# Moving the tiles that hold x's operands to other byte offsets in SBUF (linear attention, RMS norm, SiLU feed-forward)

## The chip, the cores and the metric

One Trainium2 chip, one of its cores. The metric is the device time of one execution in microseconds, the median over several runs.

## What is computed

```python
kv  = einsum('bhsd,bhse->bhde', k, v)                 # 8 x 8 heads, 576 rows, 64 wide
o   = einsum('bhsd,bhde->bhse', q, kv)
o   = o / sqrt(mean(o*o, -1) + 1e-6) * g_norm
x   = o.transpose(0, 2, 1, 3).reshape(4608, 512)
h   = x @ w_in                                         # 512 -> 2048
out = (h * sigmoid(h)) @ w_out                         # 2048 -> 512
```

Everything is float32.

## The kernel before

**Split numbers.** The large products run on TensorE in the type fp32r. To keep float32 accuracy each operand is split into an upper part in fp32r and a lower part, the rest. A product is then three matmuls into one accumulator: upper by lower, lower by upper, upper by upper. Every such matmul has a 128x128 *stationary* operand, loaded by its own LDWEIGHTS, and a *moving* operand of 512, 288 or 256 columns that streams through it. In the rows a matmul reads `out<-a,b` with its shapes `stationary moving`.

**Stages.** The 4608 tokens are nine tiles of 512 (NT = 9). `x` of a tile is stored transposed, as four chunks of 128 features by 512 tokens, each with its upper and lower part. The hidden layer is 16 blocks of 128 (NF = 16). For a block the first product (w_in, line 468 in `products`, or line 636 in `product`) has a block of w_in as stationary operand and x as moving operand; then SiLU on ScalarE and the split on VectorE make the tiles `gh` and `gl`; then the second product (w_out, line 499 in `project`) has `gh` or `gl` as stationary operand and the block of w_out (512 columns) as moving operand, into four accumulator banks.

- Token tile 0: x is in the tiles `x0` to `x3`, made by `x_part`. `x0` to `x2` lie in the three slots `spare0` to `spare2`, `x3` in the slot `late0`.
- Token tile 1: x is in the one tile `x_second`. In tiles 0 and 1 a block is 12 matmuls of line 468 (512 columns), then 12 of line 499 (512 columns).
- Token tiles 2 to 8: the first product runs as seven products of half size (Strassen-Winograd, functions `make_operand`, `product`, `pair_step`), each of six matmuls with 256 moving columns. Two blocks make one pair step, and there are 8 pair steps in each of the seven tiles, 56 in all. The moving operands of products 4, 7, 2 and 3 lie in `x_second` (it has four chunks of 4 KB for them), those of products 1, 6 and 5 in the tiles `operand4` to `operand6`, which have taken over the slots `spare0` to `spare2`. Between the products stand matmuls of line 499, in groups of three: one group after products 1 and 6, two after 5 and 4, three after 7 and 2, the rest after 3. They belong to the pair step before.
- The attention (lines 247 to 297) of the next batch is spread over the steps in between. Its output product (lines 282, 283, 284 in `mm_out`) takes three matmuls of 288 columns: stationary `kh`, `kl`, `kh`, moving `ql`, `qh`, `qh`, first on the left half of the 576 columns, then on the right half.

The order of the instructions is written out by hand in lists (`first_jobs`, `mid_jobs`, `last_jobs`), one place for each step; nothing in it depends on addresses.

**Where the tiles lie.** A tile takes a fixed stretch of bytes in each of the 128 partitions. The pools lie one after the other, `const` first, and within it the slots lie in the order in which they are first asked for, each rounded up to 32 bytes. What matters here is the start of each slot, in bytes, and its rest by 256:

```
slot                      start    rest by 256   holds
kvm0..3, kh (2 slots)      1152 ..  128          attention, kh: stationary, lines 282, 284
kl (2 slots)               4288 ..  192          stationary, line 283
x_second                   5344     224          moving, line 468 (tile 1), line 636 (products 4, 7, 2, 3)
spare0, spare1, spare2    21728 ..  224          moving, line 468 (x0..x2), line 636 (products 1, 6, 5)
late1, late0              34016 ..  224          x in float32, w_out in float32; late0 first holds x3
32 weight blocks          42208 ..  224          w_in: stationary, w_out: moving, sums of w_in: stationary
q, k, v, qh, ql           173280 .. 224          moving, lines 282 to 284: left half 224, right half 224+1152, rest 96
gh, gl                    214240 .. 224          stationary, line 499
```

Rows within the tiles are 512, 1024 or 2048 bytes apart, so that every operand of lines 468, 499 and 636 has the rest 224 as well, stationary or moving.

The diff touches `late`, which is called for the slots `late0` and `late1`, and the lines around line 106 where `x_second` is made.

Of the kernel before, what the change touches and what calls it, by code (L numbers as in the profile page):

```python
# [8 lines left out]
F32 = mybir.dt.float32  # L9
# [21 lines left out]
def linear_attention_rms_silu_ffn(  # L31
# [23 lines left out]
    B, NP, P, S = q.shape  # L55
# [9 lines left out]
    const = ctx.enter_context(tc.tile_pool(name="const", bufs=1))  # L65
# [37 lines left out]

    x_second = const.tile([P, NP, 2, TN], F32R, name="x_second")
    x_first, lates = {}, {}

    def spare(n, shape, dtype, name):
        return const.tile(shape, dtype, name=name, tag=f"spare{n}")  # L110

    def late(n, shape, dtype, name):
        if name not in lates:
            lates[name] = const.tile(shape, dtype, name=name, tag=f"late{n}")
        return lates[name]

    def x32(c, w):

        return late(c // 2, [P, 2, TN], F32, f"x32_{c // 2}")[:, c % 2, w]
# [14 lines left out]
    def full_tile(kind, f):  # L134
        if kind == "wo":
            t = late(1, [P, 2, NP * P], F32, "wo_full")[:, f % 2]
        else:
            t = tmp.tile([P, S], F32, name="full", tag="tmp")[:, :NP * P]
        fulls[kind, f] = t
        return t  # L140
# [54 lines left out]
    def x_part(t, a, c):  # L195

        if t == 1:
            return x_second[:, c, a]
        if c not in x_first:
            kind = {"shape": [P, 2, TN], "dtype": F32R, "name": f"x{c}"}  # L200
            x_first[c] = spare(c, **kind) if c < 3 else late(0, **kind)
        return x_first[c][:, a]
# [598 lines left out]
    with tc.manual_schedule():  # L801
# [4 lines left out]
        for item in ORDER.split():  # L806
            kind, n = item.rstrip("0123456789"), int(item.lstrip("wiopbg") or 0)
# [234 lines left out]
```

## Time and profile before

| | |
|---|---|
| median of 3 runs | 846.33 us (846.32 to 846.63) |
| the profiled execution | 846.25 us |
| its span, first to last instruction | 844.5 us |
| PE busy | 834.0 us, 99% of the span |
| VectorE, ScalarE, GpSimd busy | 537.1, 431.0, 290.3 us |
| clock that TensorE was granted | 1.00 of full speed throughout |

The profiled execution is 1.75 us longer than its span, and 0.08 us below the median of the runs. PE is TensorE's matmul side, PEld its weight loads, which overlap the matmuls. Matmuls overlap too: one starts while the one before drains, so the time that one takes up is the distance from its start to the start of the next, here called its *pitch*, and not its duration. In a timeline row that merges several matmuls (`x12`), the start of the next row less the start of this one, over 12, is their mean pitch.

### The profile page before, as it was taken

What the parts mean: (1) busy time and instruction counts of PE and PEld (TensorE: products, weight loads), DVE (VectorE), ACT (ScalarE), POOL (GpSimd) and SP (SyncE); (2) the same over time, 40 slices, a digit from 0 to 9 for tenths busy, and PEclk for the clock granted to TensorE, in tenths of its full rate; (3) what the DMA queues carried; (4) which work ended last, traced back from release to release, by engine and by line L of the source; (5) the groups of instructions that cost most, each with busy time, mean ns of one, the idle gap of its engine ahead of it and who ended that gap; (6) DMA issues with size and microseconds to landing.
All of it is one profiled execution on the core that took longest, in us unless ns stands there. A gap on an engine that the chain in (4) does not pass through costs nothing.

```text
span 844.5 us, 14347 instructions
## 1 busy us (share of the span) xinstructions
PE 834.0 (99%) x5454; PEld 740.3 (88%) x5454; DVE 537.1 (64%) x1067; ACT 431.0 (51%) x957; POOL 290.3 (34%) x254
## 2 busy tenths in 40 slices
PE   8999999999999999999999999999999999999998
PEld 8667888888899999999999999999999999999997
DVE  4886866774676567756766577666765763464333
ACT  4766554333664457446654465456644544454443
POOL 2776884620332223222422242223322222222220
DMA  8779011241322332232314331232211121112111
GB/s 326 304 259 358 1 57 54 98 176 61 106 76 79 134 106 101 76 131 78 111 51 134 120 116 51 85 126 83 100 50 51 50 101 50 51 51 100 51 51 50
DMA packets 33205, 89.01 MB, mean 105 GB/s; under 512 B 3824, under 2 KB 4080, under 8 KB 33136
## 3 DMA queue, kind: packets, MB, share of 16 engines
q1 hardware_dynamic: 33136, 88.10, 29.7%
q8 instruction: 43, 0.70, 0.3%
q14 instruction: 26, 0.21, 0.1%
HBM read 74.45 MB, written 13.63 MB: 104 GB/s over the span
## 4 chain that ended last, share of the span: by engine, by line
PE 94%; DMA 4%; POOL 1%; ACT 0%; issue 0%; SPq 0%
PE acc L499 46%; PE hp L636 33%; PE hp L468 9%; PE at L247 2%; DMA wo<-in_moe_w_out 1%; DMA k<-in_k 1%; DMA early_wi<-in_v 1%; PE at L284 1%; PE at L283 1%; PE at L282 1%; DMA v<-in_v 1%; PE at L499 1%; DMA wi<-in_moe_w_in 1%; PE at L280 1%; POOL wo L185 0%
## 5 line engine op out<-in xcount | busy, mean ns | idle before, releaser
L499 PE MATMUL acc<-wo,gh 128*128 128x512 f32 (+1 forms) x1152 | 357.1, 391 | 0.1
L580 POOL TENSOR_TENSOR wi<-wi,wi 128x512 fp32r<-128x512 f32 x112 | 145.2, 1297 | 420.2 <-ACT wi L579 417.2
L499 PEld LDWEIGHTS acc<-wo,gh 128*128 128x128 f32 x1152 | 201.4, 189 | 29.0 <-POOL wo L185 0.3
L499 PE MATMUL acc<-wo,gl 128*128 128x512 f32 x576 | 222.7, 387 | 0.5 <-POOL gl L479 0.5
L636 PEld LDWEIGHTS hp<-x_second,wi 128*128 128x128 f32 x1344 | 179.9, 191 | 9.0
L636 PE MATMUL hp<-x_second,wi 128*128 128x256 f32 x1344 | 187.7, 282 | 0.0
L636 PEld LDWEIGHTS hp<-operand,wi 128*128 128x128 f32 x1008 | 135.3, 190 | 9.0
L636 PE MATMUL hp<-operand,wi 128*128 128x256 f32 x1008 | 138.3, 282 | 0.0
L499 PEld LDWEIGHTS acc<-wo,gl 128*128 128x128 f32 x576 | 108.2, 188 | 24.1 <-POOL gl L479 1.0
L579 ACT CAST wi<-wi 128x512 fp32r<-128x512 f32 x112 | 69.0, 616 | 107.2 <-DMA wi<-sums_in_dram 105.3
L692 DVE TENSOR_TENSOR wi<-hp,wi 128x256 f32<-128x256 f32 x56 | 23.8, 425 | 145.9 <-PE hp L636 145.9
L643 ACT ACTIVATE gh<-gf 128x512 fp32r<-128x512 f32 x56 | 35.4, 632 | 127.4 <-DVE gf L693 127.4
L647 DVE TENSOR_TENSOR gl<-wi,gh 128x256 fp32r<-128x256 f32 x112 | 48.4, 432 | 30.7 <-ACT wi L644 28.0
L269 POOL TENSOR_TENSOR ql<-q,qh 128x576 fp32r<-128x576 f32 x24 | 34.4, 1433 | 67.2 <-ACT qh L268 56.7
L643 ACT ACTIVATE gh<-wi 128x256 fp32r<-128x256 f32 x112 | 45.9, 410 | 15.0 <-DVE wi L708 14.9
L647 DVE TENSOR_TENSOR gl<-gf,gh 128x512 fp32r<-128x512 f32 x56 | 38.7, 690 | 20.9 <-ACT gf L644 20.1
L477 ACT ACTIVATE gh<-hp 128x512 fp32r<-128x512 f32 x31 | 18.5, 597 | 61.4 <-PE hp L468 61.4
L644 ACT ACTIVATE wi<-wi 128x256 f32<-128x256 f32 x112 | 46.8, 418 | 3.5
L468 PE MATMUL hp<-x,wi 128*128 128x512 f32 x180 | 45.7, 399 | 1.4 <-POOL wi L185 1.4
L468 PE MATMUL hp<-x_second,wi 128*128 128x512 f32 x192 | 46.4, 390 | 0.0
L468 PEld LDWEIGHTS hp<-x_second,wi 128*128 128x128 f32 x192 | 35.7, 188 | 7.3
L468 PEld LDWEIGHTS hp<-x,wi 128*128 128x128 f32 x180 | 33.2, 188 | 9.0 <-POOL wi L185 1.8
(140 smaller groups left out, 1024.8 us busy)
## 6 DMA issues: line engine op xcount, KB each, us to landing
wi<-sums_in_dram SPq DMA_DIRECT2D x56, 512.0 KB, 3.3
out<-ob SPq DMA_DIRECT2D x35, 256.0 KB, 2.4
wi<-in_moe_w_in SPq DMA_DIRECT2D x16, 512.0 KB, 7.9
wo<-in_moe_w_out SPq DMA_DIRECT2D x16, 512.0 KB, 8.8
k<-in_k SPq DMA_DIRECT2D x28, 288.0 KB, 4.6
v<-in_v SPq DMA_DIRECT2D x28, 288.0 KB, 4.7
q<-in_q SPq DMA_DIRECT2D x28, 288.0 KB, 3.6
sums_in_dram<-sums SPq DMA_DIRECT2D x8, 512.0 KB, 2.6
```

Source lines behind the costliest of these rows:

```text
L247: nc.tensor.matmul(out=self.kv[h], lhsT=self.k[rows, c, :], rhs=self.v[rows, c, :], start=(start and r == 0), stop=(stop and r == 4),)
L269: nc.gpsimd.tensor_tensor(out=self.ql, in0=self.q, in1=self.qh.bitcast(F32), op=ALU.subtract)
L468: nc.tensor.matmul(out=hp[:, :TN], lhsT=w[:, a, fs], rhs=x_part(t, b, c), start=(c == 0 and i == 0), stop=(c == NP - 1 and i == 2),)
L477: nc.scalar.activation(out=gh, in_=hp[:, :TN], func=AF.Silu)
L499: nc.tensor.matmul(out=bank, lhsT=g[:, ns], rhs=w[:, a, cs], start=(f == first and i == 0), stop=(f == last and i == 2))
L579: nc.scalar.copy(out=two[:, 0], in_=raw)
L580: nc.gpsimd.tensor_tensor(out=two[:, 1], in0=raw, in1=two[:, 0].bitcast(F32), op=ALU.subtract)
L636: nc.tensor.matmul(out=out, lhsT=a_of(i, a, c), rhs=x[:, b, c], start=(n == 0), stop=(n == 5))
L643: nc.scalar.activation(out=gh[:, w], in_=x, func=AF.Silu)
L644: nc.scalar.activation(out=x, in_=x, func=AF.Silu)
L647: nc.vector.tensor_tensor(out=gl[:, w], in0=x, in1=gh[:, w].bitcast(F32), op=ALU.subtract)
L692: nc.vector.tensor_tensor(out=u3, in0=v, in1=u2, op=ALU.add)
```

## The change

Three tiles that nothing reads or writes are put between the others: 128 bytes ahead of `x_second`, 64 bytes behind it, and 64 bytes ahead of the first slot that `late` asks for.

```diff
+    def gap(n):
+
+        const.tile([P, n // 4], F32, name=f"gap{n}")
+
+    gap(128)
     x_second = const.tile([P, NP, 2, TN], F32R, name="x_second")
+    gap(64)
     x_first, lates = {}, {}
 ...
     def late(n, shape, dtype, name):
+        if not lates:
+            const.tile([P, 16], F32, name="gap_late")
         if name not in lates:
             lates[name] = const.tile(shape, dtype, name=name, tag=f"late{n}")
         return lates[name]
```

By the layout above `x_second` then starts at 5472 (rest 96), the three spare slots at 21920 and on (rest 160), and `late1` at 34272 (rest 224). All that lies behind moves up by 256 bytes and keeps its rest. No instruction is added, removed or reordered.

## Rows read from the trace of the kernel before

**Rows 1.** Page: busy time, share of the span and instructions of each engine.

```profile
PE 834.0 (99%) x5454; PEld 740.3 (88%) x5454; DVE 537.1 (64%) x1067; ACT 431.0 (51%) x957; POOL 290.3 (34%) x254
```

**Rows 2.** Page: the chain that ended last, by engine.

```profile
PE 94%; DMA 4%; POOL 1%; ACT 0%; issue 0%; SPq 0%
```

**Rows 3.** Windows: busy time by engine, then granted clock, DMA share, GB/s.

```profile
0.00:50.00 50.00, 44.16 (x325) 37.03 (x326) 34.59 (x66) 29.91 (x63) 26.86 (x43) 1.00 0.83 309
...
180.00:800.00 620.00, 620.00 (x4175) 560.20 (x4174) 389.06 (x805) 319.83 (x718) 166.93 (x127) 1.00 0.26 89
```

**Rows 4.** Groups of PE's instructions, shapes apart: count, busy us, mean ns of one.

```profile
L499 PE MATMUL acc<-wo,gh 128*128 128x512 f32 x1120 | 350.8, 394 | 0.1
L636 PE MATMUL hp<-x_second,wi 128*128 128x256 f32 x1344 | 187.7, 282 | 0.0
L636 PE MATMUL hp<-operand,wi 128*128 128x256 f32 x1008 | 138.3, 282 | 0.0
L468 PE MATMUL hp<-x_second,wi 128*128 128x512 f32 x192 | 46.4, 390 | 0.0
```

**Rows 5.** PE timeline, token tile 1: start us, us, line, operands, count.

```profile
198.99 2.88 PE L468 MATMUL hp<-x_second,wi 128*128 128x512 f32 x12
201.71 0.39 PE L499 MATMUL acc<-wo,gh 128*128 128x512 f32 x1
```

**Rows 6.** PE timeline, one pair step of a later tile.

```profile
453.04 0.63 PE L499 MATMUL acc<-wo,gh 128*128 128x512 f32 x2
...
454.43 1.59 PE L636 MATMUL hp<-operand,wi 128*128 128x256 f32 x12
455.86 0.63 PE L499 MATMUL acc<-wo,gh 128*128 128x512 f32 x2
...
456.56 0.87 PE L636 MATMUL hp<-operand,wi 128*128 128x256 f32 x6
457.26 0.88 PE L636 MATMUL hp<-x_second,wi 128*128 128x256 f32 x6
457.98 0.63 PE L499 MATMUL acc<-wo,gh 128*128 128x512 f32 x2
```

**Rows 7.** Groups of PE in 456.5 to 457.25, then 457.255 to 457.97.

```profile
L636 PE MATMUL hp<-operand,wi 128*128 128x256 f32 x6 | 0.9, 281 | 0.0
...
L636 PE MATMUL hp<-x_second,wi 128*128 128x256 f32 x6 | 0.9, 283 | 0.0
```

**Rows 8.** PE timeline: attention's output product, left half, then right half.

```profile
247.94 0.29 PE L282 MATMUL at<-ql,kh 128*128 128x288 f32 x1
248.07 0.29 PE L283 MATMUL at<-qh,kl 128*128 128x288 f32 x1
248.20 0.29 PE L284 MATMUL at<-qh,kh 128*128 128x288 f32 x1
248.34 0.63 PE L499 MATMUL acc<-wo,gh 128*128 128x512 f32 x2
...
251.09 0.29 PE L282 MATMUL at<-ql,kh 128*128 128x288 f32 x1
251.22 0.30 PE L283 MATMUL at<-qh,kl 128*128 128x288 f32 x1
251.36 0.30 PE L284 MATMUL at<-qh,kh 128*128 128x288 f32 x1
251.50 0.62 PE L499 MATMUL acc<-wo,gh 128*128 128x512 f32 x2
...
252.87 0.28 PE L636 MATMUL hp<-operand,wi 128*128 128x256 f32 x1
```

**Rows 9.** PE timeline, token tile 1, behind attention's output product.

```profile
141.97 2.92 PE L468 MATMUL hp<-x_second,wi 128*128 128x512 f32 x12
144.72 0.29 PE L282 MATMUL at<-ql,kh 128*128 128x288 f32 x1
```

**Rows 10.** One tile's instructions, 320 to 360 us: duration ns min/median/max.

```profile
L636 PE MATMUL hp<-operand,wi x65: 277/283/283, 319.8 to 356.4; 128*128 128x256 f32 x65
```

## Prediction

> **What bounds the kernel now.** I read the page's busy times first, then the chain, then the windows, then PE's groups and timelines. TensorE is busy 99% of the span [rows 1] and makes up 94% of the chain that ended last [rows 2]; the rest of the chain is mostly the DMAs of the start. Between 180 and 800 us PE is busy 620.00 of 620.00 us, at a granted clock of 1.00, while VectorE is busy 389 and ScalarE 320 us of it [rows 3]. So in three quarters of the span nothing but the pitch of the matmuls sets the time, and a nanosecond per matmul is worth microseconds: lines 636 and 468 hold 1344 + 1008 + 192 matmuls with x moving [rows 4], and 180 more with x0 to x3.
>
> The change touches no instruction, so the whole question is whether the pitch depends on where in SBUF the operands start. The reader should look at the pitch, then. In token tile 1 twelve matmuls of 512 columns take 2.72 us, 226.7 ns each [rows 5]. In the later tiles six of 256 columns take 0.72 us, 120.0 ns each (from 457.26 to 457.98) [rows 6]. The difference, 106.7 ns, is what 256 columns cost; so beside its columns each matmul takes 13.3 ns more, in both sizes alike. I call this the locked pitch. In both runs the moving and the stationary operand have the same rest of 224.
>
> The pitch is not always the locked one, and that is what the forecast rests on. (a) The six matmuls on `operand6` that follow three of line 499 have a mean duration of 281 ns, the six on `x_second` right behind them 283 [rows 7]; the shortest of a run has 277 [rows 10]. Durations move with the pitch, so these are 2 and 6 ns under the locked pitch. (b) Matmuls of 512 columns that come right behind a run of 256 columns are slower: six take 1.39 us, three take 0.70 us [rows 6], where the locked pitch makes 1.36 and 0.68. (c) Attention's three matmuls of 288 columns take 0.40 us with the rest 224 of the left half and 0.41 us with the rest 96 of the right half, with the same stationary tiles and the same work ahead of them; the line-499 matmuls behind the right half take 1.37 us for six [rows 8], not the 1.39 of (b). All 24 pairs of halves show one of two such patterns, 20 of them this one. So a moving operand's start does move the pitch, by nanoseconds.
>
> **The change part by part.** *The three gaps themselves.* They are written and read by nothing: no instruction, no wait, no transfer, cost 0. What lies behind the third gap moves by 256 bytes and keeps its rest, the weights, gh, gl, q and k among it. `x3` too: it lies in `late0`, behind the third gap, and stays at 224, so 45 of the 180 matmuls on x0 to x3 see no new rest.
>
> *256 columns, 2352 matmuls.* Their moving operands get the rests 96 and 160, against 224 of their stationary ones. No row has x moving at another rest. Below, the nearest row is (a)'s first-of-a-run, 6 ns less for every one: -14.1 us. Above, it is (c), 0.01 us in three matmuls, 3.3 ns more for every one: +7.8 us. I take (a)'s 281 against 283, -2 ns, or -4.7 us: 283 is the largest duration in [rows 10] and at once its median, so the locked pitch is the slowest that these matmuls show, and whatever breaks the lock has more room below than above.
>
> *512 columns of line 499 in the later tiles.* A pair step has four runs of them, of 3, 6, 9 and 6; 56 steps make 224 runs. Each now pays 0.02 to 0.03 us at its entry (b). Behind the right half it pays 0.01 (c). If another rest of x changed the entry in this way throughout, that would be -0.02 x 224 = -4.5 us; at worst the entry is that of [rows 9], where twelve take 2.75 us (+0.03), at no gain. I take half the gain, -2.2 us.
>
> *Tiles 0 and 1.* Here x and w_out alternate in runs of twelve, all locked [rows 5]. With different rests each switch may start a transient such as [rows 9] show behind attention's matmuls, 0.03 us. 32 blocks make 64 switches; some 48 lie behind the first 50 us, in which PE has idle time that hides them (44.16 us busy of 50 [rows 3]). 48 x 0.03 = +1.4 us, ends 0 and +1.9.
>
> *The other engines.* ScalarE and VectorE write these tiles at the new starts. Both have idle time in every window [rows 3] and PE waits for neither there; were each of the writes 2% slower it would still be hidden. If PE gets 5 us faster over 620, the others' shares rise by 1%, which makes nothing late.
>
> *Sum.* -4.7 - 2.2 + 1.4 = -5.5 us. From the profiled execution's 846.25 us, which is 0.08 us below the median of the runs, that is 840.8 us.
>
> *Two rules to weigh.* The rows show 13.3 ns beside the columns [rows 5, 6]. The Trainium skill, "TensorE: Matmul & The Clock Gate", section "Wait — 56ns, not 53.3ns?", gives a warm matmul a fixed cost of about 2.5 ns beside its columns; here the trace shows 10.8 ns more than that, and an estimate by that page, with all of it gone in 2352 matmuls, is -25.4 us, 820.9 us. Rows 8 show that the moving operand's start matters at all. The Trainium skill, "SBUF — State Buffer", section "Who interferes with whom", says that PE has two read ports, one for the moving operand and one for weight loads, independent of each other, and that PE never waits on anyone; by that the relative start could not matter and the change would be worth 0. The trace disagrees by its 0.01 us in three matmuls.
>
> **The rivals.**
> - *No effect.* What counts may be only the rest by 32 or 64, which stays what it was (224, 96 and 160 are all 32 behind a multiple of 64). For it: the locked 13.3 ns are the same for x_second, operands and weights moving, at every row inside the tiles. Against it: (c), where 224 and 96 differ. The SBUF page's two ports would give the same. Time 846.3, own range 844.7 to 848.
> - *A slower lock.* x_second at rest 96 settles on a slower pitch than at 224, as the right half does: 3.3 ns on its 1344 + 192 matmuls, +5.1 us, 851.4. It decides from the first run of x_second in tile 1, from 130 us on, and is steady through the kernel. For it: 0.41 against 0.40 us in 20 of 24 pairs. Against it: the three there never settle, their stationary rests are 128 and 192, and the run behind them gains back as much. Own range 848 to 856.
> - *Most of the 13.3 ns goes.* The fixed part comes from the moving and the stationary operand being read at equal rests, and parting them takes it away: 6.5 ns (120.0 less the 113.5 that [rows 10]'s 277 stands for) in 2352, -15.3 us, 831. For it: such a pitch does occur. Against it: only at a run's start; and three matmuls of 288 columns take 0.40 us with unequal rests, which by 106.7 ns per 256 columns leaves 13 ns each.
>
> **How the numbers follow.** The forecast case, some faster, has 0.42 (own range 836.5 to 844.5), most of it gone 0.06, no effect 0.24, slower lock 0.28. Faster by over 0.2% (1.7 us, about what a measurement of this kernel can tell from no change): 0.42 + 0.06 = 0.48; same 0.24; slower 0.28. The cases have both signs, so the range must hold them: 833 to 853.5 leaves out most of the 0.06 and the dearer third of the slower lock, 0.14 in all.
>
> **What would show it.** Right: PE's groups of line 636 fall from 282 to about 280 ns, both x_second and operand; runs of six of line 499 in the later tiles fall below 1.39 us; the twelves of tile 1 rise above 2.72 us; PE stays busy without a gap from 180 to 800 us. No effect: 2.72, 0.72 and 1.39 us unchanged. Slower lock: x_second's group of line 636 rises above 283 while operand's doesn't. If the two groups part, rests 96 and 160 differ, and the sum has to be made for each. The prediction fails altogether if gaps appear in PE's timeline, or if the groups of line 499 move by more than the entries of their runs.

## The result, and the profile after

The changed kernel takes 847.38 us, median of 20 runs (847.07 to 847.71); the kernel before took 846.25 beside it (20 runs, 845.93 to 846.63). The ratio is 1.0014, 95% interval 1.0007 to 1.0020: 1.13 us slower, which is clear of the interval but within the 0.2% that the prediction named as no change. The forecast was 840.8, 5.5 us faster. The profiled spans are 845.3 us after and 844.5 before.

The page's busy times, its chain of waits and the window from 180 to 800 us, in the columns of [rows 1 to 3]:

```profile
PE 835.2 (99%) x5454; PEld 737.2 (87%) x5454; DVE 537.2 (64%) x1067; ACT 431.0 (51%) x957; POOL 290.1 (34%) x254
...
PE 94%; DMA 4%; POOL 1%; issue 0%; ACT 0%; SPq 0%
```

```profile
180.00:800.00 620.00, 620.00 (x4171) 557.20 (x4170) 389.87 (x808) 319.93 (x718) 166.03 (x127) 1.00 0.26 89
```

PE is still busy without a gap at a granted clock of 1.00, the other engines have the same busy times, and PE has 1.2 us more. So nothing moved but the pitch, as foreseen; it only moved the other way. PE's groups, shapes apart, answer to [rows 4] (line 644 is what 636 was, 476 was 468, 507 was 499). The first row is of before, the others are of after:

```profile
L499 PE MATMUL acc<-wo,gl 128*128 128x512 f32 x560 | 218.2, 390 | 0.5 <-POOL gl L479 0.5
...
L507 PE MATMUL acc<-wo,gh 128*128 128x512 f32 x1120 | 350.5, 394 | 0.1
L507 PE MATMUL acc<-wo,gl 128*128 128x512 f32 x560 | 220.7, 394 | 0.5 <-POOL gl L487 0.5
L644 PE MATMUL hp<-x_second,wi 128*128 128x256 f32 x1344 | 188.2, 283 | 0.0
L644 PE MATMUL hp<-operand,wi 128*128 128x256 f32 x1008 | 135.3, 279 | 0.0
L476 PE MATMUL hp<-x_second,wi 128*128 128x512 f32 x192 | 47.3, 395 | 0.0
```

The two groups of line 644 part: `operand`, now at rest 160, falls from 282 to 279 ns; `x_second`, now at 96, rises from 282 to 283. The group of 512 columns on `x_second` rises from 390 to 395, that of `gl` in line 499 from 390 to 394. Tile 1 and a pair step, in the columns of [rows 5] and [rows 6]:

```profile
200.36 2.96 PE L476 MATMUL hp<-x_second,wi 128*128 128x512 f32 x12
203.15 0.63 PE L507 MATMUL acc<-wo,gh 128*128 128x512 f32 x2
```

```profile
454.65 0.63 PE L507 MATMUL acc<-wo,gh 128*128 128x512 f32 x2
...
456.04 1.54 PE L644 MATMUL hp<-operand,wi 128*128 128x256 f32 x12
457.42 0.63 PE L507 MATMUL acc<-wo,gh 128*128 128x512 f32 x2
...
458.82 0.88 PE L644 MATMUL hp<-x_second,wi 128*128 128x256 f32 x6
459.53 0.63 PE L507 MATMUL acc<-wo,gh 128*128 128x512 f32 x2
...
462.36 0.64 PE L507 MATMUL acc<-wo,gh 128*128 128x512 f32 x2
...
464.46 0.88 PE L644 MATMUL hp<-x_second,wi 128*128 128x256 f32 x6
```

Read them by the starts. The twelve of tile 1 take 2.79 us where they took 2.72. Twelve on `operand` take 1.38 (456.04 to 457.42) where they took 1.43: here the gain is. Six on `x_second` take 0.71, hardly less than the 0.72 before. The nine of line 507 behind `x_second` take 2.10 (462.36 to 464.46); nine at the locked pitch would take 2.04. The instructions on `x_second` before and after and on `operand` after, in 320 to 360 us (minimum, median and maximum duration), beside [rows 10]:

```profile
L636 PE MATMUL hp<-x_second,wi x90: 277/283/283, 322.2 to 359.9; 128*128 128x256 f32 x90
...
L644 PE MATMUL hp<-x_second,wi x78: 279/282/292, 323.7 to 358.7; 128*128 128x256 f32 x78
...
L644 PE MATMUL hp<-operand,wi x72: 276/281/281, 320.5 to 358.0; 128*128 128x256 f32 x72
```

No duration was above 283 before; now `x_second` reaches 292. By the single starts its pitch goes 117, 120, 123, 117, 120, 123 ns, a mean of 120, with durations up to 285; the 292 are 25 matmuls that stand last in a run, right ahead of attention's, at a pitch of 130. `operand` mostly goes 116, 118, 119, 116, 114, 113, 114, 113 and stays at 113.3.

### The profile page after: what moved, and what is told of

The parts are those of the page before. It is cut to its first block, busy times and chain, and to the rows that moved or that the text cites. A ratio compares the mean times of both kernels' runs of the same rounds, so it can differ in the third digit from the quotient of the medians.

```text
span 845.3 us, 14347 instructions
## 1 busy us (share of the span) xinstructions
PE 835.2 (99%) x5454; PEld 737.2 (87%) x5454; DVE 537.2 (64%) x1067; ACT 431.0 (51%) x957; POOL 290.1 (34%) x254
## 4 chain that ended last, share of the span: by engine, by line
PE 94%; DMA 4%; POOL 1%; issue 0%; ACT 0%; SPq 0%
PE acc L507 46%; PE hp L644 33%; PE hp L476 9%; PE at L255 2%; DMA wi<-in_moe_w_in 1%; DMA wo<-in_moe_w_out 1%; DMA k<-in_k 1%; PE at L291 1%; PE at L292 1%; PE at L290 1%; DMA early_wo<-in_k 1%; PE at L507 1%; DMA early_wo<-in_q 1%; PE at L288 1%; POOL wo L193 0%
## 5 line engine op out<-in xcount | busy, mean ns | idle before, releaser
L507 PE MATMUL acc<-wo,gl 128*128 128x512 f32 x576 | 225.2, 391 | 0.5 <-POOL gl L487 0.5
L644 PEld LDWEIGHTS hp<-operand,wi 128*128 128x128 f32 x1008 | 133.0, 188 | 9.3
L644 PE MATMUL hp<-operand,wi 128*128 128x256 f32 x1008 | 135.3, 279 | 0.0
```

Source lines behind the costliest of these rows:

```text
L507: nc.tensor.matmul(out=bank, lhsT=g[:, ns], rhs=w[:, a, cs], start=(f == first and i == 0), stop=(f == last and i == 2))
L644: nc.tensor.matmul(out=out, lhsT=a_of(i, a, c), rhs=x[:, b, c], start=(n == 0), stop=(n == 5))
```

## The experiments

For after and the kernels run on the whole problem I added up the pitch (the next matmul's start less this one's) over every matmul of a group, and took off the same sum of the kernel before. In us; the *difference* is from here on the moving operand's rest less the stationary one's, and the *entry* of a run is what its first matmuls take over the locked pitch:

```
group (matmuls)         after    e1     e2     e5     e8    e10    e11    e12    e14
operand, 256 (1008)     -2.90  -0.60  -1.49  -3.68  -1.42  -1.10  -1.49  -1.49  -1.20
x_second, 256 (1344)    +0.53  +0.17  -0.54  -3.62  -2.39  -1.74  -2.06  -2.05  -3.02
x, 512, tiles 0 and 1   +1.70  +1.03  +0.79  +1.91  +0.48  +0.96  +1.89  +0.79  +0.05
w_out, 512 (line 499)   +1.84  +0.76  -0.26  +4.71  +0.72  +1.15  -3.27  -3.41  -2.42
all of PE               +0.86  +1.32  -1.48  -1.07  -2.82  -0.54  -4.91  -5.98  -6.59
timed against before    +1.13  +1.30  -1.36  -1.01  -2.94  -0.70  -4.90  -6.06  -6.65
```

The last two rows agree within 0.3 us everywhere: the pitch is nearly the whole of the time.

**Each part alone, and the rests without a difference (e1 to e4).** e1 has `x_second` at 96 and the rest of before everywhere else; e2 has only the spare slots (x0 to x2, operand4 to operand6) at 160. e3 and e4 shift the stationary tiles too, by one gap ahead of everything: all at 96, all at 0.

```diff
 # e1
+    const.tile([P, 32], F32, name="gap_ahead")
     x_second = const.tile([P, NP, 2, TN], F32R, name="x_second")
+    const.tile([P, 32], F32, name="gap_behind")
 # e2
     x_second = const.tile([P, NP, 2, TN], F32R, name="x_second")
+    const.tile([P, 48], F32, name="gap_behind")
...
+        if not lates:
+            const.tile([P, 16], F32, name="gap_late")
 # e3 ([P, 32]) and e4 ([P, 8])
+    const.tile([P, 32], F32, name="gap_ahead")
     x_second = const.tile([P, NP, 2, TN], F32R, name="x_second")
```

> Only x_second moves, to the rest 96; the spare slots and all else stay at 224. Theory A (each matmul's pitch follows from the rest of its own moving operand against that of the stationary operand, so the two moves add up): line 636 on x_second +0.5 us, line 468 on x_second +0.9, line 636 on operand 0, line 499 takes +1 to +2; in all 848 to 849.5, slower than before. Theory B (what counts is that the two kinds of x tiles differ from each other, so one move alone is as good as both): operand's mean falls from 282 to 279 ns here too, 847.4. Theory C (chance, or other engines' writes): nothing moves by more than 0.3 us in any group, 846.3.

> Only the spare slots move, to the rest 160; x_second and all else stay at 224. Theory A: line 636 on operand -2.9 us (mean 279 ns), line 468 on x0 to x3 +0.8, line 636 on x_second and line 468 on it 0 (282 and 390 ns), line 499 within 0.5; in all 844 to 844.7, faster than before by 0.2%. Theory B: as with both moved, 847.4. Theory C: 846.3.

> One gap of 128 bytes ahead of x_second alone: x's tiles, the weights, q, k, v, gh and gl all get the rest 96, so moving and stationary operands of lines 468, 499 and 636 have equal rests again; only kh, kl and the masked k*v tiles keep theirs. Theory A1 (only the difference of the two rests counts): as before, 282 ns in line 636 and 2.72 us for twelve of tile 1, 846.3. Theory A2 (the moving operand's own rest counts): x_second as in the changed kernel, 283 ns and 2.77 us or more for twelve, and line 499's 512 columns too, 2000 matmuls by some 5 ns, 852 to 856.

> One gap of 32 bytes ahead of x_second: all of those operands start at a multiple of 256. Theory A1 (only the difference of the rests counts): as before, 120.0 and 226.7 ns locked, 846.3. Theory A2 (the own rest counts, above all whether an operand starts on a multiple of 64 or more): the fixed part beside the columns falls from 13.3 ns to less, in all 4400 matmuls with 256 or 512 columns; at 6.7 ns, the least that a run's first matmul showed, -29 us, 817.

Measured: e1 847.54 us against 846.24, ratio 1.0014 (1.0005 to 1.0024); e2 844.88, 0.9984 (0.9974 to 0.9993); e3 847.22, 1.0011 (1.0002 to 1.0021); e4 846.64, 1.0005 (0.9996 to 1.0015). PE's groups of e1, then of e2:

```profile
L638 PE MATMUL hp<-x_second,wi 128*128 128x256 f32 x1344 | 187.8, 282 | 0.0
L638 PE MATMUL hp<-operand,wi 128*128 128x256 f32 x1008 | 137.7, 281 | 0.0
L470 PE MATMUL hp<-x_second,wi 128*128 128x512 f32 x192 | 47.3, 395 | 0.0
```

```profile
L639 PE MATMUL hp<-x_second,wi 128*128 128x256 f32 x1344 | 187.2, 282 | 0.0
L639 PE MATMUL hp<-operand,wi 128*128 128x256 f32 x1008 | 136.7, 281 | 0.0
L471 PE MATMUL hp<-x_second,wi 128*128 128x512 f32 x192 | 46.4, 390 | 0.0
```

The expectations held in sign alone: e1 lies below Theory A's 848 to 849.5, and e2 is 0.2 us above its 844 to 844.7, with half of the gain forecast on `operand` (-1.49 us, mean 281, not 279). Theory B had e1's time, but e2 refutes it (847.4 forecast), and the groups refute Theory C. e4 can't be told from no change; e3 is 0.98 us slower, far from the 852 to 856 of Theory A2.

The two parts have opposite signs. `x_second` at 96 costs, above all in the 512 columns of tile 1 (395 against e2's 390) and behind it in line 499; the spare slots at 160 gain. The timeline of e4, tile 1 and a later tile:

```profile
198.91 2.88 PE L469 MATMUL hp<-x_second,wi 128*128 128x512 f32 x12
201.63 0.62 PE L500 MATMUL acc<-wo,gh 128*128 128x512 f32 x2
...
457.46 0.88 PE L637 MATMUL hp<-x_second,wi 128*128 128x256 f32 x6
458.18 0.63 PE L500 MATMUL acc<-wo,gh 128*128 128x512 f32 x2
```

2.72 and 0.72 us, as before, with all of it at rest 0 in place of 224. So a rest by itself does nothing to these runs; the difference counts. By the sums of pitches e3 and e4 lose 0.7 and 0.6 us in line 499 and at most 0.11 in any group on x's tiles. The loss is all behind attention's 288 columns, whose kh and kl kept their starts, so that the differences there did change.

e1 and e2 together make -0.1 us, the change +1.13: the parts don't add, against Theory A. The intervals of these times are wide for that, but the groups show it as well (line 499 has +0.76 and -0.26 by themselves, +1.84 together). The single starts show where. Twelve on `operand` behind line 499 come to 1413 ns in e2 (each 117 to 119) and to a mean of 1381 after the change (mostly 113.3 from the sixth on); nine of line 499 behind `x_second` take 27.5 ns over the locked pitch before and in e2, 44 in e1 and 52 after. The changed kernel has both cycles in itself: of its 56 runs of twelve on `operand`, 40 take 1376 or 1377 ns and 11 take 1413 or 1414. So the same matmuls with the same starts settle on one cycle or another; that the runs before decide it is the likeliest reading, but no run tried it by itself.

**One difference for every moving operand (e5 to e8).** Here w_out's blocks, which move in line 499, are shifted with x: all moving operands -64, -32, -96 or +64 from their stationary ones.

```diff
 # e5; e6, e7 and e8 have 8 and 56, 24 and 40, 48 and 16 in place of 16 and 48
+    between.tile([P, 16], F32, name="gap_between")
...
+    const.tile([P, 48], F32, name="gap_ahead")
     x_second = const.tile([P, NP, 2, TN], F32R, name="x_second")
...
-        return weights.tile([P, 2, NP * P], dtype, name=f"{kind}{f}", tag=f"{kind}{f}")
+        pool = weights_out if kind == "wo" else weights
+        return pool.tile([P, 2, NP * P], dtype, name=f"{kind}{f}", tag=f"{kind}{f}")
...
```

> The blocks of w_out get a pool of their own, so that all moving operands of lines 468, 499 and 636 (x's tiles, w_out) have the rest 160 and all stationary ones (w_in, its sums, gh, gl) 224: every load of stationary weights now differs from the running matmul's moving operand by the same -64. Theory A (the difference of rests sets the pitch): the 113.3 ns that operand's second products reached at this difference holds everywhere, 6.7 ns less in 2352 matmuls of 256 columns (-15.7 us); if the 512-column ones gain as much, another -13.7; 817 to 833. Theory D (any uniform difference locks at 13.3 ns beside the columns; only a change of difference between runs unlocks it): 282 ns in line 636 and 2.72 us for twelve of tile 1 as before, 845 to 847.

> As the kernel with -64, with all moving operands at 192, a difference of -32. Theory A: a pitch of its own, between 113 and 123 ns for 256 columns, so 830 to 853; nothing measured says which. Theory D: 845 to 847.

> As the kernel with -64, with all moving operands at 128, a difference of -96. Theory A: between the -64 of the spare slots (113 to 118 ns) and the -128 of x_second (117, 120, 123 in turn): 116 to 120 ns, 836 to 846. Theory D: 845 to 847.

> As the kernel with -64, with all moving operands at 32 of the next 256, a difference of +64. Theory A with a sign (what counts is who leads): not the -64 kernel's time, 840 to 855. Theory A without a sign (what counts is the distance alone): within 1 us of the kernel with -64. Theory D: 845 to 847.

Measured against 846.31: e5 845.30, 0.9989 (0.9980 to 0.9999); e6 851.70, 1.0064 (1.0049 to 1.0079); e7 852.05, 1.0068 (1.0053 to 1.0083); e8 843.37, 0.9964 (0.9950 to 0.9979). PE's groups of e5:

```profile
L505 PE MATMUL acc<-wo,gh 128*128 128x512 f32 x1120 | 352.4, 396 | 0.0
L642 PE MATMUL hp<-x_second,wi 128*128 128x256 f32 x1344 | 184.1, 280 | 0.0
L474 PE MATMUL hp<-x_second,wi 128*128 128x512 f32 x192 | 47.5, 396 | 0.0
```

The large gain hoped for at -64 (817 to 833) didn't come: 256 columns gain 7.3 us, but 512 columns lose 6.6 by the table. The time lies in Theory D's 845 to 847, but its rows don't: it had 282 ns and 2.72 us unchanged, and the means are 280 and 396. e6 fits Theory A's wide range; e7 was expected at 836 to 846 and missed it. By their sums of pitches, made as for the table, e6 and e7 gain only 1.3 and 3.0 us in the 256 columns and lose 6.9 and 8.9 in the 512. e8 was to be within 1 us of e5 if the sign didn't count; it is 1.9 us faster, so the sign counts too. The two widths want different differences, which no theory until then had.

**The pitch by itself (e9).** None of the reference is computed: runs of 36 matmuls with one moving tile at each difference, on two stationary tiles of the same rest in turn. It is a single execution; from 15 to 190 us PE is at a granted clock of 1.00 throughout.

> The disputed pitch by itself: none of the reference is computed; runs of 36 matmuls, each with its weight load, one moving tile for each difference of the rests (0, 16, 32, 64, 96, 128, 160, 192, 224), with 512 and with 256 columns; then with half the stationary columns (64, differences 0, 64, 128); then in bfloat16 (0, 64). Theory A (the load of the next weights and the running matmul collide in SBUF, by their difference): 512 columns 226.7 at 0, 229 at 64, 233 to 234 at 128 to 224; 256 columns 120 at 0, 113 or 118 at 64 and 192, 120 at 128; with 64 stationary columns half of the 13.3 ns beside the columns; in bfloat16 at most 3 ns beside them and no difference between 0 and 64. Theory E (the 13.3 ns are a fixed cost of changing weights, and differences only matter through the order in the kernel): the same pitch at every difference, 13.3 ns with 64 columns and in bfloat16 too.

Measured, settled pitch (the mean of the last 24 pitches of a run) in ns:

```
difference          0     16     32     64     96    128    160    192    224
512 columns     226.7  231.7  233.3  228.9  233.3  233.3  234.5  233.3  233.3
256 columns     120.0  118.6  116.7  113.3  120.0  118.8  117.4  113.3  118.3
bf16, 512       215.8                215.8
bf16, 256       109.2                109.2
```

Lines of e9's timeline, each for a run of 36 (the next start less this one, over 36, holds the entry as well):

```profile
15.14 8.32 PE L57 MATMUL f512x<-m0x,st 128*128 128x512 f32 x36
23.30 8.50 PE L57 MATMUL f512x<-m16x,st 128*128 128x512 f32 x36
31.64 8.57 PE L57 MATMUL f512x<-m32x,st 128*128 128x512 f32 x36
...
90.32 4.48 PE L57 MATMUL f256x<-m0x,st 128*128 128x256 f32 x36
94.63 4.44 PE L57 MATMUL f256x<-m16x,st 128*128 128x256 f32 x36
...
103.11 4.24 PE L57 MATMUL f256x<-m64x,st 128*128 128x256 f32 x36
107.19 4.48 PE L57 MATMUL f256x<-m96x,st 128*128 128x256 f32 x36
...
173.53 7.93 PE L57 MATMUL c512x<-b64x,stbf 128*128 128x512 bf16 x36
181.30 4.09 PE L57 MATMUL c256x<-b0x,stbf 128*128 128x256 bf16 x36
185.23 4.09 PE L57 MATMUL c256x<-b64x,stbf 128*128 128x256 bf16 x36
```

(23.30 - 15.14) / 36 is 226.7 ns, (107.19 - 103.11) / 36 is 113.3. For 512 columns difference 0 is best by 2 to 8 ns; for 256 columns 64 and 192 (that is -64) are best, by 6.7 ns against 0. bf16 pays 2.5 ns beside 213.3 and 106.7 for its columns, at 0 and at 64 alike. So Theory A's forecasts for 128 stationary columns hold within 1.2 ns, and the fixed cost of Theory E is refuted. The part of the expectation on 64 stationary columns missed: they take 228 to 230 and 116.7 ns whatever the difference, not half of what is paid beside the columns.

**The difference chosen in the kernel (e10 to e12).** e10 and e11 move `x_second` and the spare slots together, to +64 and -64. e12 is e11 with `x_second` 256 bytes longer (64 numbers, not the 64 bytes of the expectation): tile 1 (512 columns) uses it from difference 0, the later tiles' operands lie 64 bytes lower in it.

```diff
 # e10: gap_ahead [P, 16], gap_late [P, 48]; e11: [P, 48], [P, 16]; e12, beside e11's gaps:
-    x_second = const.tile([P, NP, 2, TN], F32R, name="x_second")
+    second = const.tile([P, NP * 2 * TN + 64], F32R, name="x_second")
+    x_second = second[:, 16:16 + NP * 2 * TN].rearrange("p (c a n) -> p c a n", a=2, n=TN)
+    x_operands = second[:, :NP * 2 * TN].rearrange("p (c a n) -> p c a n", a=2, n=TN)
...
-            return x_second[:, j].rearrange("p a (k n) -> p a k n", k=2)
+            return x_operands[:, j].rearrange("p a (k n) -> p a k n", k=2)
```

> x_second and the spare slots both at the rest 32, a difference of +64 to all the stationary operands; everything else at 224. Theory A: line 636 as in the kernel with +64 everywhere, -3.8 us; line 468 +0.5; line 499, whose own difference is 0 again, -0.5 to +1; 842.5 to 844.5. Theory D (order alone): 845 to 848.

> x_second and the spare slots both at the rest 160, a difference of -64; everything else at 224. Theory A: line 636 as in the kernel with -64 everywhere, -7.3 us; line 468 +1.9 (both tiles); line 499 -0.5 to +2 from its entries; 840 to 843. Theory D: 845 to 848.

> As the kernel with x at -64, but x_second is 64 bytes longer: token tile 1 uses it from the rest 224 (difference 0, best for 512 columns), the operands of the later tiles from 160 (difference -64, best for 256 columns). Theory A: line 468 on x_second 0 instead of +1.1, the rest as there: 1 us less than that kernel, 839 to 842.

Measured against 846.25: e10 845.55, 0.9992 (0.9983 to 1.0001), which can't be told from no change; e11 841.35, 0.9940 (0.9927 to 0.9954); e12 840.19, 0.9928 (0.9916 to 0.9941). A later tile of e11, then tile 1 of e12:

```profile
452.86 0.62 PE L502 MATMUL acc<-wo,gh 128*128 128x512 f32 x2
...
454.22 1.58 PE L639 MATMUL hp<-operand,wi 128*128 128x256 f32 x12
455.63 0.62 PE L502 MATMUL acc<-wo,gh 128*128 128x512 f32 x2
```

```profile
199.93 2.88 PE L473 MATMUL hp<-x_second,wi 128*128 128x512 f32 x12
202.65 0.61 PE L504 MATMUL acc<-wo,gh 128*128 128x512 f32 x2
```

At -64 six of line 499 take 1.36 us (452.86 to 454.22), the locked 6 x 226.7: the entry's 0.03 us is gone, 3.3 us over the kernel, and the 256 columns give 3.5 more. Tile 1 at difference 0 takes 2.72 again, 1.1 us less than e11. e11 and e12 fall into their ranges. e10 missed Theory A's 842.5 to 844.5: at +64 the 256 columns gain 2.8 of the 3.8 us, and line 499 loses 1.2. In isolation 256 columns took 113.3 ns at +64 and -64 alike; in the kernel -64 is better by 0.7 us in the 256 columns and by 4.4 in line 499. The kernel's runs follow on runs of another width, so this lies in the entries as far as the sums tell; it wasn't isolated.

**Which stationary operand (e13).** While a matmul moves its columns the next one's weights are being loaded (in e13 a load starts 2 to 4 ns behind the matmul ahead of its own and takes 187 or 188), so the difference could count against its own or the next one's stationary rest. None of the reference is computed: two stationary tiles whose rests are 128 bytes apart take turns. It is a single execution again, at a granted clock of 1.00 from 15 to 128 us.

> Again the pitch by itself, none of the reference computed: runs of 36 matmuls on two stationary tiles in turn, 128 bytes apart by rest, with the moving start chosen so that the difference to the matmul's own weights and to the next ones, loaded while it runs, are not the same. Theory A1 (what collides with the running matmul is the load of the next weights): own 0 and next 128 gives the pitch of 128 (512 columns 233.3, 256 columns 118.8), own 128 and next 0 that of 0 (226.7 and 120.0), own 192 and next 64 that of 64 (228.9 and 113.3), own 64 and next 192 that of 192 (233.3 and 113.3). Theory A3 (the matmul's own weights count): the other way round, own 0 and next 128 gives 226.7 and 120.0. Then 96, 64 and 32 stationary columns at the difference 0: if the cost goes with the columns loaded, the part beside the moving columns falls in step, 10, 6.7 and 3.3 ns; if it is set by how the two reads lock, it doesn't fall in step.

The first rows of three runs of 36, with 512 columns:

```profile
31.72 0.39 PE L55 MATMUL own0next128n512x<-mov,st 128*128 128x512 f32 x1
...
39.94 0.39 PE L55 MATMUL own128next0n512x<-mov,st 128*128 128x512 f32 x1
...
48.22 0.40 PE L55 MATMUL own192next64n512x<-mov,st 128*128 128x512 f32 x1
```

(39.94 - 31.72) / 36 is 228.3 ns, (48.22 - 39.94) / 36 is 230.0. Measured, settled pitch: with 512 columns, 226.7 ns where own and next difference are 0, 233.3 where both are 128, 228.3 for own 0 and next 128, 230.0 for the other order and for 64 and 192 either way; with 256 columns 120.0, 118.7, and 116.6 to 116.7 for all four mixed forms. Neither theory fits: by each, one of the first two mixed forms would take 226.7 ns, and 64 with 192 would take 113.3 with 256 columns. With 96, 64 and 32 stationary columns at difference 0 the pitch is 230.0, 230.0 and 231.7 for 512 and 116.2, 113.3 and 113.3 for 256: it rises for 512, and for 256 it falls to 113.3 and no further, so it doesn't go with the columns loaded either. With 64 stationary columns at difference 0, 256 columns took 116.7 ns in e9, where two stationary tiles took turns, and 113.3 here on one tile: the difference and the width don't fix the pitch alone. Which read the moving operand meets is left open.

**Each slot by its use (e14).** e12 with the spare slots split too: x0 to x2, which move 512 columns in tile 0, at difference 0; operand4 at -64, operand5 and operand6 at +64.

```diff
 # beside e12's edit (with + 16 in place of + 64, and without gap_late)
+    const.tile([P, 48], F32, name="gap_behind")
...
-        return const.tile(shape, dtype, name=name, tag=f"spare{n}")
+        sizes, at_x, at_operand = (1040, 1040, 1072), (16, 0, 48), (0, 16, 0)
+        at = at_operand[n] if name.startswith("operand") else at_x[n] if name[0] == "x" else 0
+        t = const.tile([P, sizes[n]], dtype, name=name, tag=f"spare{n}")[:, at:at + 1024]
...
```

> As the kernel with x at -64 and x_second split, and the three spare slots split as well: x0 to x2 at the rest 224 (difference 0), operand4 at -64, operand5 and operand6 at +64. Theory A: line 468 on x0 to x3 0 instead of +0.8 us, line 499 in token tile 0 0 instead of +0.2, line 636 on operand within 0.7 of that kernel's -1.5; 839 to 840.5, the fastest of all. If +64 enters the runs behind it worse than -64 does, line 499 gives up to 1 us back.

Measured: 839.69 against 846.34, 0.9922 (0.9909 to 0.9936), the fastest of all, faster than both kernels and within its range. Its groups:

```profile
L646 PE MATMUL hp<-x_second,wi 128*128 128x256 f32 x1344 | 184.7, 280 | 0.0
L646 PE MATMUL hp<-operand,wi 128*128 128x256 f32 x1008 | 136.9, 280 | 0.0
L478 PE MATMUL hp<-x_second,wi 128*128 128x512 f32 x192 | 46.4, 390 | 0.0
L478 PE MATMUL hp<-x,wi 128*128 128x512 f32 x180 | 45.7, 399 | 1.4 <-POOL wi L195 1.4
```

The 512 columns of tiles 0 and 1 are at their old means (390 and 399), and `x_second` behind a run on `operand` falls in with 113 ns. Line 499 gives back 1.0 us of e12's gain, as the expectation allowed for, so the time is only 0.6 us better than e12's (6.65 against 6.06).

## Why the prediction was wrong

*What bounds the kernel: right.* PE's sums of pitches and the timed differences agree within 0.3 us in the nine kernels of the table, and PE was busy without a gap from 180 to 800 us after the change too.

*Where the miss lies.* Forecast and result are 6.6 us apart: 3.8 of it in line 499 of the later tiles, 2.3 in the 256 columns, 0.5 in tiles 0 and 1. So two steps failed.

*256 columns, "-2 ns, or -4.7 us" for all 2352: this step failed.* It held that "283 is the largest duration in [rows 10] and at once its median, so the locked pitch is the slowest that these matmuls show, and whatever breaks the lock has more room below than above", and priced rests 96 and 160 alike. 160 is a difference of -64, one of the two best: -2.9 us on `operand`, 2.9 ns each, more than was taken. 96 is a difference of -128: it does break the lock, into a cycle of 117, 120 and 123 ns, whose mean is the locked 120.0; `x_second` came to +0.5 us, as the first matmul behind line 499, often 113 ns before, now takes 116 to 120, and the last one ahead of attention 130. The slowest pitch seen under one layout is no ceiling for another: 123 lay above it. In all -2.4 us, half of the term.

*Line 499 in the later tiles, -2.2 us: this step failed too, with +1.6, the wrong sign (+1.8 with tiles 0 and 1).* Only the runs of three behind `operand` gained, 4.5 ns a run. The six behind `x_second` went from 27.5 to 32.5 ns over the locked pitch and the nine from 27.5 to 52. The term was half of the gain that (c) read from [rows 8] behind attention's right half and put down to its rest of 96. But the entry is as small behind the left half, at rest 224: by the single starts of before, line 499 pays 9 to 10 ns behind either half, against 17.5 (runs of three) and 27.5 (six and nine) where no attention stands in between. So the rows showed what comes behind matmuls of 288 columns, not what another rest does. Nor had the two halves "the same work ahead of them": the left one of [rows 8] stands behind twelve matmuls of 256 columns, the right one behind six, as a wider window of before shows:

```profile
246.51 1.59 PE L636 MATMUL hp<-x_second,wi 128*128 128x256 f32 x12
...
250.38 0.87 PE L636 MATMUL hp<-x_second,wi 128*128 128x256 f32 x6
```

That an entry comes with some differences and not with others had no row. The bound "at no gain" was too kind as well. e11 and e12 show that a gain of this kind exists (-3.3 and -3.4 us), at -64 of `x_second`.

*Tiles 0 and 1, +1.4 us: near in size (+1.9), in part by luck.* x in line 468 lost 1.7 and w_out behind it 0.2 (1.6 of the 1.84 is in the later tiles). The term took a transient of 0.03 us at each switch, on x and w_out alike. Measured were 0.07 us in each twelve of tile 1, no transient but a pitch that goes 229, 238, 229, 238 to the end of the run, and 0.015 in each twelve of w_out. `x3`, which kept its rest, paid 0.14 of it, in the matmuls right behind those on `x2`.

*The rivals.* "No effect" has the nearest time, but its mechanism is refuted: e2, e8 and e11 shift starts by multiples of 64 bytes alone and change the time by 1.4 to 4.9 us. "A slower lock" had the right tile and sign, and in tile 1's 512 columns it is what happened (twelve took 2.79 us, 5.8 ns more each); on the 256 columns it wasn't. "Most of the 13.3 ns goes" gave 113.5 ns; only the runs of twelve on `operand` came near it (113.3). The four groups add up to -2.90 + 0.53 + 1.70 + 1.84 = +1.17 us; all other matmuls make -0.31, which leaves the +0.86 of pitch in the table.

*The two rules.* bf16 in e9 pays 2.5 ns beside its columns at either difference. The Trainium skill, "TensorE: Matmul & The Clock Gate", section "Wait — 56ns, not 53.3ns?", has a fixed cost of about 2.5 ns per warm matmul. The bf16 runs agree with it; F32R paid 6.7 to 21.2 ns beside its columns (113.3 less 106.7, 234.5 less 213.3), so that figure wasn't to be had for F32R at any difference tried. The Trainium skill, "SBUF — State Buffer", section "Who interferes with whom", has PE's two reads, of the moving operand and of the weights, as independent. The bf16 runs agree with that too (215.8 and 109.2 ns at 0 and 64); for F32R 120.0 against 113.3, with nothing changed but where the moving operand starts, speaks against it.

*Left open.* What in the chip makes the difference count, and against which stationary operand. That two reads collide is argued, not shown. Nor was it tried by itself what sets which of two cycles (113.3 or 117.7) a run falls into, and so how an entry goes with the difference.

## What to carry to other kernels

Where PE is busy without a gap, read the pitch of each operand and width by itself from the starts, and price a change of layout for each of them, the entries into other runs included. With F32R operands, 512 moving columns did best here at the stationary operand's rest and 256 columns 64 bytes below it, in one tile with two views where both widths use it (e12, 0.7%). Time each such layout, since the parts don't add: +64, as good by itself, was worth nothing clear in the kernel (e10). Where rows are to show what a layout does, look what else differs between them, above all what ran before. The slowest value seen in one layout bounds nothing in another.

## What had not been expected of the hardware

- The pitch of F32R matmuls goes by the difference of the two starts mod 256 bytes, in steps seen down to 16 bytes (226.7 against 231.7 ns), not by either start (2.72 and 0.72 us at rests 224 and 0 alike). That it is mod 256 shows in tile 1's 512 columns: at -96 in e7 they go through 232, 237, 238, 231, 234, 235, 233 ns, the very cycle of 160 in e9, and at -64 in e5 they take 233.3 ns, as at 192, while at 64 e8 and e9 both have 228.9.
- The best difference hangs on the width: by itself (e9) 0 for 512 columns, +64 or -64 for 256.
- The same run has more than one settled pitch: twelve on `operand` at -64 take 1376 or 1413 ns in one and the same kernel.
- Fewer stationary columns don't bring the pitch of 512 moving columns down: 226.7 ns with 128 at difference 0, 230.0 with 64, 231.7 with 32.
